# A new order of emission for the pieces of the first layer

## The chip, the cores and the metric

The kernel runs on one core of one Trainium2 chip. The metric is the device time of one execution in microseconds (us); the median of three runs is given. Times within an execution come from one profiled execution and count from its first instruction.

## The reference

Three stages follow each other. The first is a gated delta rule over 4 batches, 8 heads, 768 steps and 48 dimensions; its output becomes a matrix x of 3072 tokens by 384. The other two are MLP layers over that matrix.

```python
for t in range(S):
    y[:, :, t] = einsum('bhd,bhde->bhe', q[:, :, t], state)
    v_old = einsum('bhde,bhd->bhe', state, k_n[:, :, t])
    state = state + b[t] * einsum('bhd,bhe->bhde', k_n[:, :, t], v[:, :, t] - v_old)
h = maximum(x @ w_in, 0);  x = (h * h) @ w_out              # 384 -> 2048 -> 384
gate = 1 / (1 + exp(-(x @ w_gate)));  out = (gate * (x @ w_val)) @ w_out2   # 384 -> 1536 -> 384
```

The weights of both MLP layers arrive as 64-bit floats, which the kernel itself turns into pairs of 32-bit numbers.

## The kernel before

"First layer" is what one long list orders: the delta rule and the squared-ReLU MLP together, with the conversion of their weights. The sequence of 768 steps is cut into 12 chunks of 64 steps, handled in 6 groups (g = 0 to 5) of two chunks (st = 0 and 1). A group gives 512 token rows, on which the MLP runs with 16 slices of 128 hidden units.

Every piece of work is a Python function, and `ORDER` (lines 38 to 89) is a string of 961 tokens, "name,arguments". The loop `for token in ORDER.split(): run(token)` (line 775) calls them one after the other under a manual schedule. Nothing else orders the work: each engine, and SP's queue of DMAs, executes its own instructions in the order of emission, and an instruction whose input or buffer isn't ready holds back all that stand behind it on the same engine. The tokens:

- Loads, issued on SP: `kn`, `kt`, `kc`, `kz`, `q`, `v`, `k2` (keys, queries and values of a chunk in several layouts, two buffers each), `f` (64-bit weights of hidden slice f, 768 KB), `li` and `lw` (low parts of a slice's weights for the first and second product, read back from DRAM, three buffers each). `sl` stores the low part of a slice, `z` moves the rows of a chunk into token order by DMA, `po` stores a finished group.
- Norms: `sq` (ACT), `sm` (VectorE, L325), `no` (VectorE with a square root on ACT, L331 to L348). `sv` scales v on POOL (L312).
- Delta rule inside a chunk, on TensorE with evictions on VectorE or ACT: `a` (scores among keys, L363 and L367), `p` (scores against queries, L383 or L398); then the inversion of the triangular blocks: `ti` (memsets on POOL, a 32 by 32 transpose on VectorE, L439 and L441), `r,g,i` (three rows of the inversion each, on VectorE, L447 to L477), `to` and `t1` (transposes, L480 and L483), `ja`, `jb`, `jc` (joins of 16-row blocks, groups 0 and 1), `n` and `w` (joins of 32-row blocks).
- Across chunks, one after the other: `ks` (product with the state, L566 to L578), `t` (L584), `y` (output, L620 and L622), `s` (new state, L597 and L607). `x` splits the rows into a high and a low part (L125 on ACT, L126 on VectorE); the row buffer xr is single, so `z` of the next chunk waits for `x` of the one before.
- Weights of slice f: `hi` (ACT), `b` (VectorE, L148 and L152), `b2` (VectorE, L157 and L161), `lo` (POOL, L168), `ch` (ACT, L214), `cl` (POOL, L218). The buffer between `hi` and `cl` is double, so `hi` of a slice waits for `cl` of the one two before. `w2,i,k` are the same steps for weights of the second layer.
- MLP, n = 16 g + f: `h,n` is 9 matmuls of 512 columns (L681) and three ACT passes; `g,n` a subtraction on VectorE (L704); `o,n` 9 matmuls (L719), which need `g,n`. `h,16 g` needs both `x` of its group.
- `d,n` issues n matmuls that only keep TensorE busy.

PSUM holds three banks for the attention pieces; most of these take two. After the list, a loop ends the first layer (slices 82 to 95), and a second one computes the gated layer.

Of the kernel before, what the change touches and what calls it, by code (L numbers as in the profile page):

```python
# [59 lines left out]
sv,2,1 a,3,0 h,23 w,2,1 g,22 w2,0,3 lw,23 t,2,0 ti,3 ti,3,3 li,24 k2,2,1 o,21 h,25 w2,0,4 lw,22 g,23 y,2,0  # L60
ti,3,1 w2,1,0 q,2,1 lw,24 w2,1,1 r,3,0 g,25 kc,2,1 o,22 r,3,1 r,3,2 lw,27 h,24 g,24 s,2,0 o,23 li,27 h,27 li,26
r,3,3 g,27 ks,2,1 o,24 v,3,0 h,26 lw,25 z,2,0 r,3,4 x,2,0 o,25 li,28 t,2,1 g,26 h,28 y,2,1 kn,4,1 lw,26 o,26
li,34 li,29 sq,4,1 r,3,5 o,27 r,3,6 w2,0,5 h,29 r,3,7 lw,28 g,28 k2,3,0 sv,3,0 z,2,1 g,29 s,2,1 w2,1,2 w2,1,3
lw,29 li,30 h,30 x,2,1 kz,3,0 o,28 o,29 g,30 v,3,1 li,31 r,3,8 li,32 lw,30 kc,3,0 lw,32 p,3,0 h,31 g,31 r,3,9
r,3,10 h,32 w2,1,4 g,32 to,3 lw,33 o,30 h,34 kz,3,1 p,3,1 li,33 lw,31 o,31 h,33 sm,4,1 n,3,0 ks,3,0 w2,2,0
w2,2,1 li,36 g,33 kt,4,1 kt,4,0 no,4 li,35 t1,3 lw,34 o,32 a,4,0 w2,1,5 n,3,1 h,36 lw,35 o,33 g,34 k2,3,1 h,35
w2,2,2 a,4,1 w,3,0 w2,2,3 o,34 t,3,0 lw,36 g,35 g,36 li,37 w,3,1 ti,4 w2,2,4 ti,4,1 kc,3,1 li,38 ti,4,3 po,1
h,37 g,37 r,4,0 r,4,1 y,3,0 w2,3,0 o,35 h,38 r,4,2 o,36 g,38 s,3,0 lw,37 li,40 w2,3,1 r,4,3 h,40 r,4,4 sv,3,1
li,39 o,37 g,40 h,39 lw,38 z,3,0 g,39 o,38 kn,5,1 ks,3,1 sq,5,0 x,3,0 w2,2,5 lw,39 lw,40 li,42 w2,3,2 q,4,0
w2,3,3 h,42 o,39 sq,5,1 o,40 q,3,1 g,42 t,3,1 li,44 r,4,5 v,4,0 li,41 h,41 g,41 k2,4,0 lw,41 lw,44 li,43 r,4,6  # L70
y,3,1 h,43 g,43 r,4,7 lw,42 kc,5,1 o,41 o,42 sv,4,0 h,44 li,45 kz,4,0 g,44 li,46 lw,43 w2,3,4 p,4,0 w2,4,0 z,3,1
r,4,8 x,3,1 h,46 r,4,9 g,46 o,43 w2,3,5 h,45 g,45 s,3,1 o,44 li,50 w2,4,1 w2,4,2 lw,47 lw,45 r,4,10 w2,4,3 h,50
to,4 li,47 o,45 lw,46 h,47 g,47 t1,4 o,46 g,50 kz,4,1 li,49 p,4,1 sm,5,0 li,48 w2,4,4 n,4,0 lw,49 o,47 lw,50
sm,5,1 h,48 w2,4,5 lw,48 w2,5,0 w,4,0 g,48 kt,5,0 ks,4,0 h,49 o,48 li,51 li,52 lw,51 no,5 w2,5,1 t,4,0 g,49 h,52
o,49 kt,5,1 w2,5,2 li,53 w2,5,3 h,51 w2,5,4 a,5,0 po,2 g,51 v,4,1 li,55 sv,4,1 n,4,1 o,50 g,52 lw,54 a,5,1
w2,5,5 w,4,1 h,53 g,53 o,51 li,56 h,56 lw,52 o,52 ti,5 ti,5,3 w2,6,0 w2,6,1 g,56 w2,6,2 y,4,0 lw,53 kc,4,1
w2,6,3 o,53 li,54 q,4,1 z,4,0 ti,5,1 h,54 r,5,0 g,54 li,58 s,4,0 h,55 li,59 o,54 h,59 w2,6,4 w2,6,5 r,5,1 lw,56
g,55 r,5,2 lw,55 li,57 w2,7,0 w2,7,1 r,5,3 r,5,4 o,55 h,57 g,57 o,56 lw,57 w2,7,2 lw,58 h,58 lw,60 li,60 ks,4,1
o,57 g,59 h,60 g,58 t,4,1 o,58 v,5,0 li,61 li,66 lw,59 g,60 x,4,0 h,61 r,5,5 y,4,1 q,5,0 g,61 k2,5,0 li,62 o,59
w2,7,3 h,62 kz,5,0 r,5,6 o,60 p,5,0 g,62 li,65 lw,61 o,61 z,4,1 x,4,1 lw,64 w2,7,4 li,63 h,63 lw,62 w2,7,5 r,5,7  # L80
g,63 r,5,8 h,66 lw,63 o,62 li,64 li,70 kc,5,0 h,64 g,66 g,64 o,63 h,65 o,64 li,68 h,68 ks,0,0 g,65 lw,65 o,65
li,67 lw,66 h,67 g,67 o,66 w2,8,0 li,69 h,69 g,68 r,5,9 lw,67 w2,8,1 sv,5,0 o,67 h,70 li,74 r,5,10 lw,68 to,5
g,69 w2,8,2 o,68 g,70 k2,4,1 li,72 lw,71 lw,69 s,4,1 n,5,0 po,3 t1,5 lw,75 o,69 h,72 li,71 lw,70 w2,8,3 ks,5,0
n,5,1 w,5,0 li,73 w2,8,4 h,71 t,5,0 o,70 w2,9,0 g,72 h,74 y,5,0 g,71 o,71 h,73 g,73 q,5,1 li,76 w2,8,5 kz,5,1
p,5,1 li,75 lw,73 lw,72 w,5,1 o,72 o,73 lw,74 g,74 v,5,1 w2,9,1 w2,9,2 sv,5,1 w2,9,3 s,5,0 li,78 h,75 z,5,0 g,75
w2,9,4 w2,9,5 h,76 g,76 o,74 ks,5,1 o,75 w2,10,0 w2,10,1 h,78 lw,76 x,5,0 li,77 t,5,1 o,76 h,77 g,77 y,5,1 li,82
li,79 lw,78 h,79 lw,77 lw,79 o,77 g,78 li,81 w2,10,2 z,5,1 w2,10,3 g,79 li,80 x,5,1 w2,10,4 w2,10,5 w2,11,0
lw,80 o,78 lw,81 o,79 k2,5,1 h,80 lw,82 h,81 g,80 li,83 w2,11,1 w2,11,2 g,81 w2,11,3 w2,11,4 po,4
# [1210 lines left out]
```

## Time and profile before

| | |
|---|---|
| median of 3 runs | 1071.47 us (1062.65 to 1074.42) |
| the profiled execution | 1073.17 us, of which the span from the first to the last instruction is 1071.4 us |
| mean granted TensorE clock | 0.984 |
| TensorE busy | 1003.6 us (94%) |
| VectorE busy | 772.5 us (72%) |
| ACT, POOL busy | 463.2 us, 200.7 us |
| end of the first layer (its last o in the chain) | some 633 us |

Busy times are those of the engine's instructions; a matmul's end is modelled and overlaps the next. The granted clock is a share of full speed (1 is 2.4 GHz, 0.5 is 1.2 GHz). "Issue" as a releaser means that the engine waited for nothing that the profile shows. In the rows below, a bracket behind an instruction is the engine's idle time ahead of it and what ended that. A matmul of 32-bit floats counts as two instructions in attention pieces.

### The profile page before, as it was taken

The numbers are of one execution on the slowest core, as the hardware profiler recorded it, in microseconds if no ns is written. First come the engines' busy times: TensorE is split into PE (matmuls) and PEld (weight loads), VectorE is DVE, ScalarE is ACT, GpSimd is POOL, SyncE is SP. The second block draws the span as 40 slices with busy tenths as digits, with TensorE's granted clock in tenths as the row PEclk, the third lists the DMA queues.
The fourth block names the chain that finished last, engine by engine and source line by source line (L and its number), as shares of the span: only waits on it lengthen the run. The fifth ranks groups of instructions, "written<-read, shape, count | busy, mean of one in ns | idle before, by whom it ended". The sixth has DMA issues, their size and how long they took to land.

```text
span 1071.4 us, 27395 instructions
## 1 busy us (share of the span) xinstructions
PE 1003.6 (94%) x11607; PEld 821.8 (77%) x11611; DVE 772.5 (72%) x1460; ACT 463.2 (43%) x763; POOL 200.7 (19%) x157
## 2 busy tenths in 40 slices
...
GB/s 283 173 209 198 194 202 210 193 200 156 188 197 135 247 171 208 178 178 170 136 159 251 262 226 243 187 162 123 216 160 131 99 126 89 89 133 171 110 3 57
DMA packets 81803, 182.78 MB, mean 171 GB/s; under 512 B 22032, under 2 KB 54928, under 8 KB 77072
## 3 DMA queue, kind: packets, MB, share of 16 engines
...
## 4 chain that ended last, share of the span: by engine, by line
PE 81%; DVE 6%; issue 2%; DMA 2%; ACT 1%; POOL 1%; SPq 1%; DVEq 0%; ACTq 0%; POOLq 0%
PE h L681 18%; PE o L719 18%; PE gx L1140 12%; PE gy L1140 11%; PE o L1019 10%; PE r L1199 2%; DMA il<-w1d 2%; PE att L553 1%; PE att L584 1%; PE att L620 1%; PE att L566 1%; PE att L538 1%; PE att L622 1%; PE att L377 1%; PE att L363 1%
## 5 line engine op out<-in xcount | busy, mean ns | idle before, releaser
L704 DVE TENSOR_TENSOR gl<-gg,gh 128x512 fp32r<-128x512 f32 x96 | 73.5, 773 | 94.3 <-ACT gg L698 94.0
L695 ACT ACTIVATE gg<-h 128x512 f32<-128x512 f32 x96 | 57.4, 598 | 181.7 <-PE h L681 171.9
L719 PE MATMUL o<-gh,il 128*128 128x512 f32 x288 | 113.8, 395 | 1.2 <-DMA il<-w1d 1.2
L1019 PE MATMUL o<-gh,wo 128*128 128x512 f32 x270 | 93.0, 394 | 0.0
L719 PE MATMUL o<-gh,w1h 128*128 128x512 f32 x216 | 87.8, 406 | 0.0
L681 PE MATMUL h<-xhi,il 128*128 128x512 f32 x288 | 84.1, 401 | 2.3 <-DMA il<-w1d 2.3
L719 PE MATMUL o<-gl,w1h 128*128 128x512 f32 x216 | 85.7, 397 | 0.0
L1140 PE MATMUL gx<-xa,wg 128*128 128x512 f32 x288 | 76.7, 395 | 2.1 <-DVE valB L1052 1.2
L1140 PE MATMUL gy<-xa,wg 128*128 128x512 f32 x288 | 76.2, 393 | 0.0
L681 PEld LDWEIGHTS h<-xhi,il 128*128 128x128 f32 x288 | 55.6, 194 | 15.8 <-DMA il<-w1d 3.6
L681 PE MATMUL h<-xhi,w1h 128*128 128x512 f32 x216 | 66.3, 417 | 0.0
L1140 PEld LDWEIGHTS gx<-xa,wg 128*128 128x128 f32 x288 | 53.6, 188 | 16.4 <-DVE gateB L1052 2.3
L719 PEld LDWEIGHTS o<-gh,il 128*128 128x128 f32 x288 | 54.7, 190 | 12.6 <-DMA il<-w1d 1.9
L1140 PEld LDWEIGHTS gy<-xa,wg 128*128 128x128 f32 x288 | 53.7, 188 | 13.0 <-DVE gateC L1052 0.4
L681 PE MATMUL h<-xlo,w1h 128*128 128x512 f32 x216 | 62.0, 396 | 0.0
L698 ACT ACTIVATE gg<-gg 128x512 f32<-128x512 f32 x96 | 60.7, 632 | 3.1
L697 ACT ACTIVATE gh<-gg 128x512 fp32r<-128x512 f32 x96 | 60.7, 632 | 3.1
L168 POOL TENSOR_TENSOR y<-raw 128x768 f32<-128x768 f32 x12 | 19.7, 1643 | 217.7 <-DVE raw L161 167.3
L1019 PEld LDWEIGHTS o<-gh,wo 128*128 128x128 f32 x270 | 50.7, 188 | 11.9
L470 DVE TENSOR_TENSOR tt<-tt,tmp 128x40 f32<-128x40 f32 (+7 forms) x208 | 52.2, 285 | 1.5 <-DVE tmp L463 0.2
L1019 PE MATMUL o<-gl,wo 128*128 128x512 f32 x135 | 53.2, 394 | 0.0
L463 DVE TENSOR_TENSOR tmp<-xi,tt 128x40 f32<-128x40 f32 (+7 forms) x208 | 51.0, 279 | 1.3
...
## 6 DMA issues: line engine op xcount, KB each, us to landing
...
```

The lines of the kernel that those rows point to most:

```text
L168: nc.gpsimd.tensor_tensor(out=t, in0=c["t"], in1=c["raw"][:, :, 0].bitcast(F32), op=ALU.add)
L463: nc.vector.tensor_tensor(out=tv[i], in0=xi[:, 0:j, j].unsqueeze(2).to_broadcast([128, j, n]), in1=tt[:, j, lo:hi].unsqueeze(1).to_broadca ...
L470: nc.vector.tensor_tensor(out=tt[:, 0:j, lo:hi], in0=tt[:, 0:j, lo:hi], in1=tv[i], op=ALU.subtract)
L681: nc.tensor.matmul(out=ps[:, cs], lhsT=w[:, kc * 128:kc * 128 + 128], rhs=x[:, kc, cs], start=(i == 0 and kc == 0), stop=(i == 2 and kc == ...
L695: nc.scalar.activation(out=gg, in_=ps, func=ACTF.Relu)
L697: nc.scalar.activation(out=gh, in_=gg, func=ACTF.Square)
L698: nc.scalar.activation(out=gg, in_=gg, func=ACTF.Square)
L704: nc.vector.tensor_tensor(out=gl, in0=gg, in1=gh.bitcast(F32), op=ALU.subtract)
L719: nc.tensor.matmul(out=po[m], lhsT=w[:, cs], rhs=x, start=(f == 0 and i == 0), stop=(f == NF1 - 1 and i == 2),)
L1019: nc.tensor.matmul(out=po2[g, m], lhsT=w, rhs=x, start=start, stop=stop)
L1140: nc.tensor.matmul(out=ps, lhsT=a, rhs=c, start=k == 0 and u == us[0], stop=k == 2 and u == us[-1],)
L1199: nc.tensor.matmul(out=po_m, lhsT=x[:, cs], rhs=w, start=f == 0 and i == 0, stop=f == NF2 - 1 and i == 2)
```

## The change

The string `ORDER` is replaced by another order of the same 961 tokens, each as often as before. The first 31 tokens are the same (line 39 and line 40 up to r,0,4). The functions behind the tokens, buffers and the code after the list are the same. The parts that are spoken of below, old lines and then new ones:

```diff
 d,1 kn,0,0 sq,0,0 kn,0,1 sm,0,0 kt,0,0 sq,0,1 be sm,0,1 no,0 kt,0,1 d,1 a,0,0 cj kn,1,1 q,0,1 kc,0,1 f,0 a,0,1
-kn,1,0 k2,0,1 cs ti,0 ti,0,1 ti,0,3 kt,1,1 r,0,0 r,0,1 r,0,2 r,0,3 r,0,4 f,1 d,1 f,2 hi,1 hi,0 to,0 p,0,1 b,0
-b2,0 d,1 lo,0 sq,1,0 sq,1,1 ja,0,1 kc,0,0 sm,1,1 t1,0 ch,0 cl,0 ja,0,0 jb,0,0 b,1 k2,0,0 v,0,0 b2,1 hi,2 kt,1,0
-v,0,1 lo,1 ch,1 sm,1,0 kn,2,0 b,2 q,0,0 p,0,0 jc,0,0 sl,0 f,3 lw,0 cl,1 n,0,0 b2,2 kn,3,1 sl,1 no,1 a,1,0 sq,2,0
-lo,2 ch,2 sm,2,0 cl,2 li,0 sq,3,1 sv,0,0 hi,3 w,0,0 q,1,0 b,3 jb,0,1 f,5 hi,5 b2,3 lo,3 t,0,0 sm,3,1 n,0,1 f,4
-sl,2 b,5 b2,5 lo,5 a,1,1 ch,3 cl,3 v,1,0 hi,4 b,4 jc,0,1 kn,2,1 b2,4 li,2 s,0,0 w,0,1 sv,0,1 lo,4 ti,1 kt,2,0
-f,8 ks,0,1 ti,1,1 sv,1,0 ti,1,3 r,1,0 sl,3 ch,4 r,1,1 k2,1,0 y,0,0 f,6 z,0,0 r,1,2 cl,4 t,0,1 ch,5 x,0,0 sl,4
-y,0,1 kn,3,0 r,1,3 r,1,4 hi,6 to,1 kc,2,0 lw,2 z,0,1 d,1 b,6 x,0,1 b2,6 cl,5 lo,6 f,7 s,0,1 d,2 ja,1,1 hi,7 lw,1
-b,7 sq,2,1 sl,5 t1,1 ch,6 sq,3,0 cl,6 b2,7 h,0 ja,1,0 li,1 hi,8 g,0 h,1 lo,7 kc,1,0 sm,2,1 ch,7 b,8 jb,1,1 h,2
-o,0 li,4 f,9 g,1 o,1 sl,6 cl,7 b2,8 lo,8 li,3 kt,2,1 ks,1,0 hi,9 ch,8 h,3 li,5 f,10 sl,7 lw,3 g,2 q,1,1 b,9 h,5
-no,2 jb,1,0 cl,8 b2,9 n,1,1 hi,10 g,3 lw,6 lo,9 o,2 li,6 h,4 b,10 ch,9 f,11 g,4 o,3 sl,8 p,1,0 cl,9 hi,11 kn,4,0
-b2,10 sm,3,0 sq,4,0 lw,4 lw,5 jc,1,1 lo,10 b,11 ch,10 li,7 g,5 h,6 kc,1,1 o,4 sl,9 a,2,1 li,8 b2,11 n,1,0 f,12
-cl,10 jc,1,0 hi,12 lo,11 ch,11 li,9 g,6 b,12 sl,10 cl,11 o,5 w,1,0 a,2,0 h,7 b2,12 g,7 o,6 f,13 hi,13 b,13 w,1,1
-b2,13 li,10 lo,12 t,1,0 lw,7 o,7 lo,13 ti,2 ti,2,3 ti,2,1 sl,11 lw,9 ch,12 cl,12 h,9 v,1,1 sv,1,1 h,8 g,8 y,1,0
...
-g,15 p,2,1 h,17 g,16 g,17 w2,0,1 o,15 r,2,7 v,2,0 li,18 r,2,8 h,18 li,20 lw,17 g,18 k2,2,0 li,21 o,16 o,17 h,20
-li,19 h,19 r,2,9 lw,18 g,20 g,19 o,18 h,21 r,2,10 sv,2,0 lw,19 kt,3,1 kn,5,0 q,2,0 lw,20 o,19 to,2 t1,2 li,25
-kc,4,0 ks,2,0 n,2,0 v,2,1 li,23 o,20 no,3 n,2,1 li,22 a,3,1 h,22 kt,3,0 g,21 q,3,0 lw,21 po,0 w,2,0 w2,0,2
...
+kn,1,0 k2,0,1 cs ti,0 ti,0,1 ti,0,3 kt,1,1 r,0,0 r,0,1 r,0,2 r,0,3 r,0,4 sq,1,0 v,0,0 sv,0,0 to,0 q,0,0 v,0,1
+sv,0,1 hi,0 d,1 d,1 f,1 kt,1,0 hi,1 k2,0,0 d,1 p,0,1 b,0 b2,0 ja,0,0 sm,1,0 lo,0 ch,0 ja,0,1 kc,0,0 cl,0 b,1 f,2
+hi,2 kn,3,1 sl,0 t1,0 sq,1,1 b2,1 lo,1 ch,1 cl,1 p,0,0 b,2 jb,0,0 b2,2 sq,3,1 f,3 hi,3 lo,2 ch,2 jb,0,1 n,0,0
+jc,0,0 sm,1,1 b,3 b2,3 no,1 f,4 n,0,1 sl,1 sm,3,1 cl,2 f,5 hi,5 b,5 w,0,0 a,1,1 kn,3,0 lo,3 sq,3,0 sl,2 ch,3
+cl,3 jc,0,1 q,1,0 li,1 hi,4 t,0,0 sm,3,0 kc,1,0 b2,5 li,0 b,4 w,0,1 b2,4 lo,4 ch,4 a,1,0 f,6 sl,3 kn,2,1 ti,1
+cl,4 ti,1,1 f,7 lo,5 s,0,0 sq,2,1 sl,4 hi,6 ks,0,1 b,6 ch,5 lw,0 ti,1,3 y,0,0 v,1,1 z,0,0 t,0,1 cl,5 sl,5 r,1,0
+r,1,1 r,1,2 x,0,0 y,0,1 b2,6 d,2 lw,3 r,1,3 lo,6 s,0,1 r,1,4 f,8 z,0,1 kn,2,0 x,0,1 hi,7 li,4 ch,6 cl,6 to,1
+sq,2,0 b,7 b2,7 hi,8 p,1,0 k2,1,0 h,0 lo,7 ja,1,0 b,8 f,9 t1,1 ch,7 b2,8 h,1 ja,1,1 sl,6 cl,7 g,0 g,1 hi,9 h,4
+li,5 sm,2,0 lo,8 ch,8 b,9 kt,2,0 o,0 f,10 sl,7 cl,8 b2,9 li,2 lo,9 jb,1,0 lw,1 kt,2,1 sm,2,1 o,1 q,1,1 hi,10
+ch,9 sl,8 jb,1,1 lw,2 n,1,0 b,10 b2,10 no,2 li,3 h,2 g,2 a,2,0 cl,9 f,11 lo,10 n,1,1 g,4 hi,11 b,11 ch,10 h,3
+v,1,0 o,2 jc,1,0 sl,9 cl,10 b2,11 jc,1,1 a,2,1 g,3 lw,4 f,12 w,1,0 hi,12 sl,10 b,12 h,5 sv,1,0 ks,1,0 li,6 lo,11
+ch,11 b2,12 cl,11 lw,5 o,3 kc,1,1 li,8 w,1,1 t,1,0 ti,2 ti,2,1 f,13 lo,12 hi,13 h,8 b,13 b2,13 kz,2,0 p,1,1 li,7
+o,4 lo,13 ch,12 g,8 h,6 sl,11 g,5 li,9 ti,2,3 lw,6 g,6 cl,12 y,1,0 ch,13 r,2,0 o,5 kc,2,0 f,14 p,2,0 hi,14 b,14
+b2,14 o,6 lw,8 r,2,1 h,7 g,7 s,1,0 r,2,2 sl,12 h,9 g,9 lw,7 z,1,0 x,1,0 v,2,0 o,7 o,8 r,2,3 sv,1,1 li,10 cl,13
...
+h,15 g,15 li,16 w2,0,0 h,16 r,2,9 r,2,10 kt,3,0 w2,0,1 h,17 s,1,1 to,2 li,21 g,16 lw,15 o,15 lw,17 li,19 h,19
+ks,2,0 n,2,0 li,18 o,16 g,17 po,0 no,3 a,3,0 t1,2 n,2,1 h,18 g,18 o,17 kt,3,1 a,3,1 lw,18 w,2,0 g,19 w2,0,2 h,21
+lw,19 w2,0,3 w2,0,4 w,2,1 ti,3 q,2,1 li,23 ti,3,1 li,20 kc,3,0 v,3,0 ti,3,3 r,3,0 kn,4,0 r,3,1 t,2,0 lw,23 o,18
+o,19 lw,21 kz,3,0 g,21 lw,20 y,2,0 w2,1,0 h,20 li,22 g,20 r,3,2 w2,1,1 kc,2,1 s,2,0 h,23 o,20 li,25 li,24 r,3,3
...
+ks,3,0 n,3,0 v,3,1 w2,2,5 o,31 w,3,0 sm,4,1 no,4 a,4,0 li,34 g,33 q,3,0 h,34 g,34 lw,32 o,32 a,4,1 w,3,1 ti,4
```

Some of what differs: sv,0,0 and sv,0,1 stand ahead of to,0 and hi,0. POOL's order lo,3 lo,5 cl,3 sv,0,1 lo,4 becomes lo,3 cl,3 lo,4 ti,1 cl,4 lo,5. ja,1,1 stands behind h,1 rather than ahead of h,0, and p,1,0 ahead of h,0. The conversion of slices 13 and 14, the transposes and first rows of group 2 and p,1,1 and p,2,0 stand ahead of g,7. Loads of group 3 are spread over more tokens.

## Rows read from the trace of the kernel before

**Rows 1.** Busy time by stretch: the first layer in three parts (engines PE, PEld, DVE, ACT, POOL)
```profile
core 0: us, PE busy (x) PEld busy (x) DVE busy (x) ACT busy (x) POOL busy (x), PEclk, DMA share, GB/s
0.00:98.30 98.30, 53.09 (x1926) 47.87 (x1930) 80.38 (x136) 35.45 (x57) 39.43 (x46) 0.96 0.70 211
98.30:210.30 112.00, 107.41 (x2103) 86.74 (x2092) 100.18 (x168) 64.59 (x104) 43.08 (x24) 0.94 0.68 208
210.30:640.00 429.70, 420.99 (x5750) 344.35 (x5749) 291.98 (x681) 228.13 (x373) 44.45 (x34) 0.98 0.64 189
```

**Rows 2.** Waits of VectorE from 31.4 to 156 us, and its busy time there
```profile
engine line waited for: us in total, times, longest us
DVE y L148 <- ACT wt L143: 4.4, 3, 3.5
DVE gl L704 <- ACT gg L698: 2.9, 2, 1.5
DVE rn L336 <- ACT n L334: 2.6, 2, 2.1
DVE ks L574 <- PE att L566: 2.1, 1, 2.1
DVE pm L398 <- PE att L392: 1.5, 2, 1.3
DVE am L367 <- PE att L363: 1.4, 1, 1.4
...
31.40:156.00 124.60, 97.05 (x2891) 83.65 (x2893) 105.80 (x149) 64.22 (x106) 54.74 (x30) 0.92 0.63 193
```

**Rows 3.** Timeline up to the first MLP product (start us, us, engine, line)
```profile
90.62 0.96 DVE L126 TENSOR_TENSOR xlo<-xr,xhi 128x768 fp32r<-128x768 f32 x1
...
95.89 0.83 ACT L125 CAST xhi<-xr 128x768 fp32r<-128x768 f32 x1 [7.58 <-DMA xr<-yt]
...
97.15 1.26 PE L499 MATMUL att<-t,am 32*16 32x16 f32 x128 [8.20 <-DVE t L480]
...
98.34 1.65 PE L681 MATMUL h<-xhi,w1h 128*128 128x512 f32 x3
```

**Rows 4.** Groups of VectorE by line: xcount, busy us, mean ns, idle before
```profile
L152 DVE SCALAR_TENSOR_TENSOR wt<-wt,y 128x768 uint32<-128x768 uint32 x16 | 16.8, 1052 | 1.5
L148 DVE TENSOR_SCALAR y<-wt 128x768 uint32<-128x768 uint32 x16 | 15.4, 963 | 4.4 <-ACT wt L143 4.4
L157 DVE TENSOR_SCALAR y<-wt 128x768 uint32<-128x768 uint32 x16 | 10.7, 670 | 0.3
L161 DVE SCALAR_TENSOR_TENSOR raw<-raw,y 128x768 f32<-128x768 uint32 x19 | 18.2, 959 | 0.7
L470 DVE TENSOR_TENSOR tt<-tt,tmp 128x40 f32<-128x40 f32 (+7 forms) x208 | 52.2, 285 | 1.5 <-DVE tmp L463 0.2
L463 DVE TENSOR_TENSOR tmp<-xi,tt 128x40 f32<-128x40 f32 (+7 forms) x208 | 51.0, 279 | 1.3
L439 DVE STREAM_TRANSPOSE xi<-am 128x1024 f32<-128x1024 f32 x6 | 12.0, 1998 | 3.8 <-PE att L553 3.7
L383 DVE TENSOR_TENSOR pm<-att,mask 128x512 f32<-128x512 f32 x16 | 10.2, 681 | 0.5 <-PE att L377 0.5
```

**Rows 5.** Timeline: a row of the inversion beside a POOL instruction
```profile
86.94 1.82 POOL L218 TENSOR_TENSOR wl<-wt,w1h 128x768 fp32r<-128x768 f32 x1 [5.66 <-DMA w1d<-wl]
87.04 1.87 DVE L450 TENSOR_TENSOR tmp<-xi,tt 128x126 f32<-128x126 f32 x1
```

**Rows 6.** Timeline and chain: g,7; o,7's start; two h; one s piece
```profile
154.96 1.04 DVE L704 TENSOR_TENSOR gl<-gg,gh 128x512 fp32r<-128x512 f32 x1 [1.46 <-ACT gg L698]
...
157.14 0.50 PE L719 MATMUL o<-gh,w1h 128*128 128x512 f32 x1
...
159.48 4.08 PE h L681 x18
...
167.78 1.15 PE L597 MATMUL att<-u,k 64*64 64x48 f32 x64
```

**Rows 7.** The stop inside a,3,1, and the busy table around it
```profile
237.08 1.87 PE L363 MATMUL att<-kt 48*64 48x64 f32 x63 [2.42 <-issue]
...
225.00:236.00 11.00, 9.66 (x220) 7.79 (x218) 9.02 (x20) 6.42 (x10) 2.53 (x3) 1.00 1.00 274
235.00:240.00 5.00, 2.92 (x66) 2.61 (x67) 1.03 (x2) 0.68 (x2) 0.00 (x0) 0.75 0.14 47
```

More of the change, by code (lines that the diff above doesn't have):

```diff
@@ L49 @@
-no,2 jb,1,0 cl,8 b2,9 n,1,1 hi,10 g,3 lw,6 lo,9 o,2 li,6 h,4 b,10 ch,9 f,11 g,4 o,3 sl,8 p,1,0 cl,9 hi,11 kn,4,0
-b2,10 sm,3,0 sq,4,0 lw,4 lw,5 jc,1,1 lo,10 b,11 ch,10 li,7 g,5 h,6 kc,1,1 o,4 sl,9 a,2,1 li,8 b2,11 n,1,0 f,12
-cl,10 jc,1,0 hi,12 lo,11 ch,11 li,9 g,6 b,12 sl,10 cl,11 o,5 w,1,0 a,2,0 h,7 b2,12 g,7 o,6 f,13 hi,13 b,13 w,1,1
-b2,13 li,10 lo,12 t,1,0 lw,7 o,7 lo,13 ti,2 ti,2,3 ti,2,1 sl,11 lw,9 ch,12 cl,12 h,9 v,1,1 sv,1,1 h,8 g,8 y,1,0
-kz,2,0 f,14 ch,13 g,9 r,2,0 hi,14 b,14 h,10 lw,8 s,1,0 sl,12 o,8 o,9 b2,14 cl,13 sm,4,0 ks,1,1 z,1,0 li,11 x,1,0
```

62 lines of the change are left out of this document (30 added, 32 removed).

## The prediction

> **What bounds the kernel now.** I read the busy time by stretch first, then what TensorE and VectorE waited for, and last the timeline around the first MoE product. In the busy table the reader is to see three stretches of the first layer [rows 1]. Up to 98.3 us, where token h,0 starts, TensorE is busy 53.1 of 98.3 us: 45 us are lost, and VectorE (80.4 us) carries the stretch. From 98.3 to 210.3 us TensorE loses 4.6 us of 112 and its granted clock averages 0.94; VectorE is busy 100 of 112 us, so both are near their ends. From 210.3 to 640 us TensorE is busy 421.0 of 429.7 us. The list moves no work in or out, so its effect on the end of the layer is the change in TensorE's lost time: its idle time, and what a lower clock stretches.
>
> VectorE's waits between 31.4 and 156 us add up to 4.4 + 2.9 + 2.6 + 2.1 + 1.5 + 1.4 = 14.9 us [rows 2]. The rest of its 18.8 us of idle time there (124.6 - 105.8), 3.9 us, is gaps between its 149 instructions, 0.026 us each, which no order takes away.
>
> **How h,0 comes to start at 98.34 us** [rows 3]. x,0,0's subtraction starts at 90.62 and takes 0.96 us; it frees the one xr buffer, the row DMAs z,0,1 go out, and x,0,1's cast starts at 95.89 and takes 0.83 us: 5.1 us from the end of one to the end of the other, 96.72. h,0 could start there, but ja,1,1 stands ahead of it on TensorE and waits for the transpose to,1 until 97.15.
>
> **The change, part by part.** *The start.* To r,0,4 the two lists are the same tokens. Between there and x,0,0 the new list gives VectorE sm,3,0 and b,6 more and sm,2,0 less: b is one tensor_scalar and one scalar_tensor_tensor, 0.96 + 1.05 = 2.0 us [rows 4]. It takes away two waits: POOL's order lo,3 lo,5 cl,3, which held cl,3, and so hi,4, back until b2,5 was done (3.5 us of the row y <- wt), becomes lo,3 cl,3 lo,4; and no,1 comes after b,3, so that the square root on ACT should be reached (2.1 us of the row rn <- n) [rows 2]. I take 5 us of waits gone and 1 us new (ks,0,1 follows s,0,0's eviction on ACT, which now stands behind ch,4). So xlo(0,0) ends at 91.6 + 2.0 - 5 + 1 = 89.6 and h,0 starts at 94.7, for ja,1,1 is no longer ahead of it: p,1,0 is, whose inputs are loaded long before. That is 3.6 us earlier. If POOL's lo and ch still hold hi,4 back, it is 98; if nothing is waited for, 93.7.
>
> *scale_v moved forward.* sv,0,0 and sv,0,1 on POOL go from behind cl,2 and cl,3 to a place ahead of lo,0, so that they run once v has landed, which I take to be beside group 0's rows on VectorE. A row that meets a POOL tensor_tensor can wait for its end: L450 took 1.87 us beside one of 1.82 us, where its neighbours take some 0.3 [rows 5]. Two such meetings cost up to 2 x 1.6 = 3.2 us, or nothing if v lands while the transposes before the rows run; the meetings that the same two had in their old places, of the same price at most, go. The balance lies between -3.2 and +3.2 us; I take +1, since the rows are many and short, and the old neighbours longer.
>
> *From h,0 to o,7: VectorE's work is pulled ahead.* This speaks against the change. Before g,7, counted from the start, the new list has on VectorE all that the old one has, and besides ti,2 ti,2,1 ti,2,3 (3 x 2.0 us), b and b2 of chunks 13 and 14 (2 x (0.96 + 1.05 + 0.67 + 0.96) = 7.3), p,1,1 and p,2,0 (4 x 0.68 = 2.7), g,8 (0.8) and r,2,0 r,2,1 (2 of the 44 row tokens of groups 2 to 5 that share 51.0 + 52.2 us: 4.7): 21.5 us [rows 4]. 40 instructions add 1.0 us of gaps. g,7 ended at 156.0 us [rows 6]. With all waits gone and w new ones it ends at 156.0 + 21.5 + 1.0 + 1 - 14.9 + w = 164.6 + w. TensorE, for its part, has six tokens more done before o,7 (h,8 h,9 at half of 4.08 us each, p,1,1 p,2,0 s,1,0 at 1.1, y,1,0 with twice the matmuls at 2.1: 9.5 us). The old list started o,7 at 157.1 [rows 6], so it had that much done at 166.6. The gain at o,7 is thus 166.6 - 164.6 - w = 2.0 - w: the 3.6 us of the start are mostly paid back, because o,7 needs g,7. w lies between 0 and the 14.9 of before; as VectorE now runs behind TensorE rather than ahead of it, its inputs are there when it comes, and I take w = 0.5, near the lower end. Gain 1.5 us. Past o,7 TensorE has no wait of the same kind to 200 us, so this gain stays.
>
> *The stop at 234 us.* TensorE stood 2.42 us inside a,3,1, waiting for nothing that the profile shows, while the DMA engines were busy at a share of 1.00; its granted clock was 0.75 in the 5 us around it, a mean over its two levels (1.2 and 2.4 GHz) [rows 7]. In the old list the loads kt,3,0 and q,3,0 and the store po,0 of a group's output stand within eight tokens there, and n,2,1 a,3,1 follow ks,2,0 n,2,0 with one o between. In the new one kt,3,0 is issued before h,17 and q,3,0 not before g,33, and a,3,0 n,2,1 come with h,18 and o,17 behind them. I take this stop as gone: 2.4 us, and 5 x 0.25 = 1.3 us of clock, 3.7 us. Ends: nothing, if stops fall anywhere in instruction-dense pieces (the new list has 16 places with two or more attention pieces in a row after h,17, the old one 15), and minus as much again if one more comes. The Trainium skill, "Runtime: NRT & Kernel Launch", section "Instruction fetch mechanics", has the sequencer refill instructions in blocks through its own DMA queue, a cost that it calls mostly hidden. The stop in a busy DMA stretch goes against "hidden"; by the page there would be nothing for the list to move, and the sum would end 3.7 us higher.
>
> *The rest.* From o,20 on each pair is a reshuffle with the same sets within a few us; loads il keep three buffers, and their waits (some 0.3 to 1 us each) I cost at nothing, hidden by TensorE's queue of h and o; without that cover each late one costs 1 us. The second layer has no edit.
>
> **Sum.** 1.5 + 3.7 = 5.2 us. The profiled execution took 1073.2 us (span 1071.4), which gives 1068.0; the median of the runs shown, 1071.5, lies 1.7 us lower, so I forecast **1066** for a median.
>
> **Rivals.**
> 1. *The stops go altogether.* From 210 to 640 us 8.7 us are idle and the clock's mean of 0.98 stretches some 8 us more [rows 1]. If the new spacing removes three quarters of these 17 us (12.7) and w is 0 (2.0), the time is 1071.5 - 14.7, near 1057. For it: only a handful of stops hold most of that time. Against it: 16 dense places for 15.
> 2. *Nothing moves.* The stops stay, the start is paid back whole: 1071. For it: the lost time of the old list before o,7 is VectorE's, and VectorE gets more to do there. Against it: 14.9 us of waits are to be had, and the new order does the waiting work later.
> 3. *VectorE becomes the bound between o,5 and o,16: slower.* Mechanism: the rows and weight chunks pulled ahead of g,7 are themselves late, because hi and ch on ACT wait for POOL, as cl,3 did. Every us that VectorE waits before g,7 then goes to the end, for TensorE has nothing else queued. With w = 14 (the waits of before, moved) the gain at o,7 is -12; with the stop at 234 us staying, the time is 1071.5 + 12 = 1083; with half of the waits, w = 7, it is 1076. It decides from w = 2 on if no stop goes, from w = 5.7 if the one does. For it: the share of VectorE is already 0.89 there, and the slack of every g before its o shrinks. Against it: a stall of VectorE in the old list often was one for TensorE, which ran ahead less.
>
> **How the numbers follow.** The forecast (1061 to 1071) has 0.44, rival 1 0.29, rival 2 0.11, rival 3 0.16. A measurement of this kernel can tell about 1% from no change, 10.7 us (its three runs spread over 11.8 us). Faster by over 1%, below 1060.8: most of rival 1 (0.25) and the forecast's edge (0.06), 0.31. Slower by over 1%, above 1082.2: half of rival 3 and a little, 0.10. Within: 0.59. The range runs from 1053 (rival 1 with nearly all 17 us) to 1079 (rival 3 with w near 9); about 0.1 lies on each side. The likeliest case's own range is 1061 to 1071.
>
> **What would show it.** Right: h,0 starts at 93.7 to 96 us; in VectorE's waits the row y <- wt falls from 4.4 to under 1.5 us before o,7; o,7 starts within 4 us of 164.6; VectorE's busy share from h,0 to o,7 is above 0.93; the stop inside a,3,1 is gone and the clock holds 1.00 there. Wrong: h,0 at 98 us or later (the start's step); o,7 after 168 us (rival 3); a stop of over 2 us in another dense piece (the late step); or idle time of TensorE from 210 to 640 us under 4 us (rival 1).

## The result, and the profile after

The new list takes **1084.3 us** (median of six runs, 1081.6 to 1086.9); beside it the list of before took 1069.5 us (1062.7 to 1077.3). The ratio is 1.0123, with an interval of 1.0093 to 1.0153. That is some 13 us slower, where I forecast 1066 us: outside the range, and on the side that I gave a chance of 0.10. The profiled execution took 1084.7 us, with a span of 1083.0.

The busy table of the new list, cut at the same three tokens as [rows 1] and with its columns (h,0 now starts at 102.5 us, o,15 at 226.0):

```profile
0.00:102.50 102.50, 55.54 (x1865) 48.90 (x1865) 86.32 (x137) 39.06 (x62) 42.03 (x47) 0.61 0.72 209
102.50:226.00 123.50, 108.98 (x2158) 86.50 (x2156) 109.53 (x202) 61.43 (x101) 41.81 (x23) 0.93 0.65 190
226.00:652.00 426.00, 420.00 (x5754) 343.94 (x5751) 291.46 (x646) 228.07 (x373) 43.31 (x34) 0.99 0.64 189
```

At o,15 both lists have given TensorE the same work, and the new one gets there 15.7 us later. TensorE's idle time up to there grew by 11.7 us: from 45.2 to 47.0 us ahead of h,0, and from 4.6 to 14.5 us between h,0 and o,15. Its busy time grew by 4.0 us (160.5 to 164.5) for the same matmuls, those that ran at a lower granted clock among them. Behind o,15 the new list is no worse: 6.0 us idle, 8.7 before. The loss is made by 226 us, and most of it between h,0 and o,15.

The granted clock up to h,0 was 0.61 in this execution and 0.96 before, but the loss doesn't hang on that: of the six runs of the new list, the two with a mean clock of 0.950 and 0.953 took 1084.7 and 1081.6 us, and the four with 0.984 to 0.987 took 1082.9 to 1086.9 us.

What TensorE waited for from 102.5 to 226 us (columns: us in total, times, longest):

```profile
PE o L719 <- DVE gl L704: 8.2, 4, 3.2
PE h L681 <- DMA il<-w1d: 2.6, 1, 2.6
PE att L553 <- issue: 2.3, 1, 2.3
```

The first row did not exist before: four times an o stood and waited for VectorE's g. VectorE itself, from 31.4 us to the end of g,7 (181.7 us now, 156.0 before), which answers to [rows 2]:

```profile
DVE y L148 <- ACT wt L143: 3.4, 2, 2.8
DVE ks L574 <- PE att L566: 1.9, 1, 1.9
DVE am L367 <- PE att L363: 1.8, 1, 1.8
DVE rn L336 <- ACT n L334: 0.6, 2, 0.3
DVE wt L152 <- DVE y L148: 0.5, 1, 0.5
DVE xlo L126 <- DMA w1s<-in_w_dram: 0.2, 1, 0.2
...
31.40:181.73 150.33, 113.04 (x3296) 94.97 (x3296) 137.27 (x178) 74.95 (x123) 62.09 (x36) 0.73 0.61 187
```

Its waits fell from 14.9 to 8.4 us, but its busy time up to the same token rose from 105.8 to 137.3 us. That is 31.5 us more, where I had counted 21.5. Where the other ten come from is seen in the same instructions' mean times. From 31.4 us to g,7, the list of before:

```profile
L157 DVE TENSOR_SCALAR y<-wt 128x768 uint32<-128x768 uint32 x13 | 9.0, 695 | 0.2
L704 DVE TENSOR_TENSOR gl<-gg,gh 128x512 fp32r<-128x512 f32 x8 | 7.5, 932 | 2.9 <-ACT gg L698 2.9
```

and the new list:

```profile
L157 DVE TENSOR_SCALAR y<-wt 128x768 uint32<-128x768 uint32 x15 | 13.6, 907 | 0.3
L704 DVE TENSOR_TENSOR gl<-gg,gh 128x512 fp32r<-128x512 f32 x9 | 12.3, 1380 | 0.0
L470 DVE TENSOR_TENSOR tt<-tt,tmp 128x31 f32<-128x31 f32 (+5 forms) x6 | 4.8, 804 | 0.2
L463 DVE TENSOR_TENSOR tmp<-xi,tt 128x31 f32<-128x31 f32 (+5 forms) x6 | 1.6, 260 | 0.1
```

The same subtraction of g took 0.93 us on the mean before and takes 1.38 now. The timeline just ahead of g,7 shows what stretches a row of the solve:

```profile
170.89 1.84 POOL L218 TENSOR_TENSOR wl<-wt,w1s 128x768 fp32r<-128x768 f32 x1 [2.12 <-DMA w1d<-wl]
170.90 1.91 DVE L470 TENSOR_TENSOR tt<-tt,tmp 128x60 f32<-128x60 f32 x1
...
173.13 0.25 DVE L470 TENSOR_TENSOR tt<-tt,tmp 128x87 f32<-128x87 f32 x1
...
177.77 1.84 POOL L168 TENSOR_TENSOR wt<-wt,raw 128x768 f32<-128x768 f32 x1 [5.04 <-DVE raw L161]
177.91 1.83 DVE L470 TENSOR_TENSOR tt<-tt,tmp 128x112 f32<-128x112 f32 x1
...
181.78 0.50 PE L719 MATMUL o<-gl,w1h 128*128 128x512 f32 x1 [3.21 <-DVE gl L704]
```

A row that takes 0.25 us alone takes 1.8 to 1.9 us when it starts beside a POOL tensor_tensor of 1.84 us. Two of them stand ahead of g,7 and cost 3.2 us together, and the last line shows TensorE waiting 3.21 us for that g. It is the meeting of [rows 5], more often and in a place where TensorE waits for it. The Trainium skill, "SBUF — State Buffer", section "Who interferes with whom", says that a VectorE instruction with two SBUF inputs and a GpSimd (POOL) instruction that reads SBUF lock each other out, the later one for the whole of the other; the 1.91 us beside 1.84 agree with that.

The start, which answers to [rows 3]:

```profile
92.93 0.96 DVE L126 TENSOR_TENSOR xlo<-xr,xhi 128x768 fp32r<-128x768 f32 x1
...
95.58 1.81 DVE L454 TENSOR_TENSOR tt<-tt,tmp 128x120 f32<-128x120 f32 x1
...
97.97 0.83 ACT L125 CAST xhi<-xr 128x768 fp32r<-128x768 f32 x1 [6.43 <-DMA xr<-yt]
98.51 1.70 DVE L607 TENSOR_TENSOR state<-state,att 128x384 f32<-128x384 f32 x3
99.11 3.47 PE L392 MATMUL att<-q,kc 48*64 48x64 f32 x60 [6.52 <-DVE state L607]
...
102.51 1.65 PE L681 MATMUL h<-xhi,w1h 128*128 128x512 f32 x3
```

x,0,0's subtraction comes at 92.93 (90.62 before), and x,0,1's cast ends at 98.80, 4.9 us behind the subtraction's end, as the 5.1 of [rows 3] let expect. But p,1,0, which the new list has ahead of h,0, stands 6.52 us: it needs two of the three PSUM buffers of the attention, and s,0,1 holds two until VectorE has added them to the state, behind a row stretched to 1.81 us. h,0 starts at 102.51. In the profiles of four kernels below whose tokens up to h,0 are the same, it starts at 100.3 to 101.5 us, so up to 2.2 of the 4.2 us belong to this one execution.

### The profile page after: what moved, and what is told of

It is laid out like the page before. It is cut to its first block, busy times and chain, and to the rows that moved or that the text cites. A ratio compares the mean times of both kernels' runs of the same rounds, so it can differ in the third digit from the quotient of the medians.

```text
span 1083.0 us, 27402 instructions
## 1 busy us (share of the span) xinstructions
PE 1006.2 (93%) x11611; PEld 821.8 (76%) x11611; DVE 785.8 (73%) x1460; ACT 463.6 (43%) x763; POOL 201.1 (19%) x157
## 4 chain that ended last, share of the span: by engine, by line
PE 76%; DVE 15%; issue 3%; DMA 3%; ACT 1%; SPq 1%; POOL 1%; DVEq 0%; ACTq 0%; POOLq 0%
PE h L681 16%; PE o L719 16%; PE gx L1140 11%; PE gy L1140 11%; PE o L1019 10%; PE r L1199 2%; PE att L553 1%; PE att L363 1%; DVE xi L441 1%; DVE tt L470 1%; PE att L584 1%; DVE gl L704 1%; PE att L566 1%; DVE y L148 1%; DVE wt L152 1%
## 5 line engine op out<-in xcount | busy, mean ns | idle before, releaser
L719 PEld LDWEIGHTS o<-gl,w1h 128*128 128x128 f32 x216 | 41.0, 190 | 18.6 <-DVE gl L704 9.9
L463 DVE TENSOR_TENSOR tmp<-xi,tt 128x40 f32<-128x40 f32 (+7 forms) x208 | 53.3, 289 | 1.4
```

The lines of the kernel that those rows point to most:

```text
L463: nc.vector.tensor_tensor(out=tv[i], in0=xi[:, 0:j, j].unsqueeze(2).to_broadcast([128, j, n]), in1=tt[:, j, lo:hi].unsqueeze(1).to_broadca ...
L719: nc.tensor.matmul(out=po[m], lhsT=w[:, cs], rhs=x, start=(f == 0 and i == 0), stop=(f == NF1 - 1 and i == 2),)
```

## The experiments

Times of one batch are compared with the list of before on the same chip; medians of before were 1068.9 to 1070.4 us. In four kernels (the g's moved, the solve moved together with p,2,0, p,1,0 moved, the late part alone) the line numbers of the profile are one lower.

**Only the g's moved.** Theory V was that VectorE's total is the bound, theory G that the g's merely stand too late.

```diff
-... h,0 lo,7 ja,1,0 b,8 ... h,1 ja,1,1 sl,6 cl,7 g,0 g,1 ...
+... h,0 g,0 lo,7 ja,1,0 b,8 ... h,1 g,1 ja,1,1 sl,6 cl,7 ...
```

> The new list with eight g tokens (0, 1, 3, 4, 5, 6, 7, 8) moved up to stand right behind their own h; nothing else moves. Theory V (VectorE's total up to g,15, its instructions stretched beside POOL included, sets the stretch from h,0 to o,15): the four waits of o for gl, 8.2 us, shrink but the work that stood ahead of the g's is late next; o,15 starts at 222 to 226 us (226.0 in the new list) and the time is 1081 to 1085 us. Rival G (only the g's stand too late): the 8.2 us go whole and are not paid back; o,15 near 217 us, time 1075 to 1077 us.

Measured: 1082.8 us, ratio 1.011 (1.0072 to 1.0149), 1.6 us under the new list and within its noise. TensorE's waits from 101.5 to 227 us:

```profile
PE o L718 <- DVE gl L703: 3.1, 1, 3.1
...
PE att L510 <- DVE xi L482: 1.3, 1, 1.3
...
PE att L498 <- DVE t L479: 1.1, 1, 1.1
PE att L583 <- DVE v L577: 0.9, 2, 0.7
```

The wait for g fell from 8.2 to 3.1 us, and waits for VectorE's other results took its place (xi, t, v). o,15 came at 227.2 us, 1.2 us behind the new list's. G falls: the g's place is not the cause, the work that somebody must wait for is.

**The group-2 solve put back**, first with p,2,0, then alone.

```diff
-o,3 ... t,1,0 ti,2 ti,2,1 ... ti,2,3 ... r,2,0 o,5 kc,2,0 f,14 p,2,0 ... o,6 lw,8 r,2,1 h,7 g,7
+o,7 ti,2 ti,2,1 ti,2,3 o,8 r,2,0 ... o,9 r,2,1 r,2,2 ... g,12 r,2,3 r,2,4 ...
```

> The new list with the group-2 solve put back behind the products it was pulled ahead of: ti,2 ti,2,1 ti,2,3 behind o,7, r,2,0 to r,2,6 behind o,8 to g,13, p,2,0 behind g,11. Theory V: VectorE has some 12 us less ahead of g,7, fewer short rows meet POOL's tensor_tensors, and TensorE has no more waits for gl from o,5 to o,7; but the rows have to be done before o,16 all the same, so about half is paid back there: o,7 at 168 to 172 us (178.0), time 1075 to 1080 us. Rival G as in the other run (only the place of the g's matters, and they get free here too): 1075 to 1077 us with o,7 near 170. Rival S (the loss is made before h,0 and by the half clock there): o,15 stays within 2 us of 226, time 1082 to 1085 us.

> The new list with the group-2 solve alone put back (ti,2 ti,2,1 ti,2,3 behind o,7, r,2,0 to r,2,6 behind o,8 to g,13); p,2,0 stays in its new place. Theory B (VectorE's work pulled ahead of the g's is what costs): o,7 starts near 174 us as it did with p,2,0 moved too, the wait of 8.9 us for p,2,0's buffers does not come, and of the 5 to 6 us won at o,9 about half is left at o,15: time 1077 to 1081 us. Rival T (VectorE's total up to g,15 is what costs, wherever its parts stand): o,15 stays at 224 to 228 us, time 1082 to 1086 us.

With p,2,0 moved: 1090.4 us, ratio 1.0188 (1.0148 to 1.0227), worse than the new list and outside what each of the three theories gave. o,7 started at 174.5 us (178.0 in the new list) and o,9 at 182.1 us (188.9), but then a new wait gave back more than that:

```profile
196.77 1.28 DVE L382 TENSOR_TENSOR pm<-att,mask 128x512 f32<-128x512 f32 x2
197.50 1.94 PE L583 MATMUL att<-v,t 64*64 64x48 f32 x60 [8.90 <-DVE pm L382]
```

t,1,1 needed PSUM buffers that p,2,0 held, whose eviction stood on VectorE behind the rows just put there. With the solve alone moved: 1081.5 us, ratio 1.0117 (1.0086 to 1.0147). o,9 came at 182.6 us, 6.3 us earlier, but o,15 at 224.9, only 1.1 earlier, as rival T has it, and TensorE's wait for g was 9.3 us. Work moved behind one product is in the way of the next: it is the total that counts. The median lies 2.8 us under the new list's, between the two forecasts, but the ratio, taken on the same chip, only 0.0006 under.

**p,1,0 behind h,0.**

```diff
-hi,8 p,1,0 k2,1,0 h,0 ... o,2 jc,1,0
+hi,8 k2,1,0 h,0 ... o,2 p,1,0 jc,1,0
```

> The new list with p,1,0 moved from ahead of h,0 to behind o,2, near its old place. TensorE stood 6.5 us in it, waiting for VectorE's eviction of s,0,1, which holds two of the three PSUM buffers. Theory V: h,0 starts at 99 us instead of 102.5 (the cast of x,0,1 ends at 98.8), but g,7 and o,15 hang on VectorE, so o,15 moves by 2 us at most and the time is 1082 to 1085 us. Rival S (the late start of h,0 is carried to the end): time 1079 to 1081 us.

Measured: 1089.6 us, ratio 1.019 (1.0146 to 1.0234). Both missed. h,0 starts at 96.65 us, earlier than before the change, and nothing is won: TensorE then waits inside h,0 for VectorE's half of x.

```profile
96.65 1.65 PE L680 MATMUL h<-xhi,w1h 128*128 128x512 f32 x3 [6.72 <-ACT xhi L124]
...
102.28 1.65 PE L680 MATMUL h<-xlo,w1h 128*128 128x512 f32 x3 [2.70 <-DVE xlo L125]
```

So h,0 is done at 103.9 us. In the run with the new start and the loads of before (below), p,1,0 stands 6.53 us in its place ahead of h,0, and h,0 is done at 103.85 us (its last three matmuls start at 103.00 and take 0.85 us). The 6.5 us that p,1,0 stood thus cost nothing by themselves there, and an earlier h,0 is not a gain as long as VectorE is late. Why the list with p,1,0 moved is 5 us worse than the new list stays open; its profiled run was the fastest of its four (1082.3 us).

**The late part alone.** The list of before up to o,15, then the new order.

```diff
 ... g,17 w2,0,1 o,15
-r,2,7 v,2,0 li,18 r,2,8 h,18 ...
+v,2,0 k2,2,0 sv,2,0 q,2,0 r,2,7 r,2,8 ...
```

> The list of before up to o,15, and behind it what is left, in the order of the new list. In the two profiles o,15 starts 15.7 us later in the new list and the first layer ends 12.4 us later, so the late part would be 3.3 us shorter. Theory L (the late part of the new list is better by itself): the time is 3 us under the kernel before, ratio 0.995 to 0.999. Rival N (the late part only had slack to catch up after a late VectorE): ratio 0.999 to 1.003. Rival W (instruction-dense places of the new list cost more stops): ratio above 1.003.

Measured with 12 runs: 1070.7 us, ratio 1.0005 (0.9976 to 1.0033). The late part is worth less than some 3 us either way. Rival N fits this best: the 3.3 us that the new list made up in its profile would then be slack behind a late o,15. That there is such slack is argued, not shown.

**VectorE relieved, in both lists.** First POOL's work on the chunks nearly taken away, so that little stretches VectorE; then VectorE's own b left out for ten chunks.

```diff
-out=t, in0=c["t"], in1=c["raw"][:, :, 0].bitcast(F32), op=ALU.add
+out=t[:, 0:32], in0=c["t"][:, 0:32], in1=c["raw"][:, 0:32, 0].bitcast(F32), op=ALU.add
...
-nc.gpsimd.tensor_tensor(out=wl_t[f], in0=wt_t.pop(f), in1=w1h[f].bitcast(F32), op=ALU.subtract)
+wl_t[f] = w1h[f]
... (the second relief, in b)
+if not all_:  # chunks 6 to 15
+    return
```

> The list of before, with POOL's work on the weight chunks nearly gone: the add of lo runs over 32 of 768 columns, and cl's subtraction is left out (the low part of w1 that is stored is a copy of the high part), so the products use other numbers. It is the base for the next run. All theories: VectorE's short instructions are no longer stretched to 1.8 us beside a POOL tensor_tensor (14.8 us of it from h,0 to o,15), and time falls by 0 to 12 us against the kernel before.

> The same two edits in the new list (lo's add over 32 columns, cl's subtraction left out, so the products use other numbers). Theory V (the new list loses because VectorE, the bound from h,0 to o,15, is stretched by 11 us more beside POOL): the new list is at most 5 us behind the list of before with the same edits. Rival B (VectorE's backlog as such: g's, PSUM evictions and the solve stand behind work pulled ahead, stretched or not): still 8 to 15 us behind. Rival P (TensorE's own stops for nothing that shows and the half clock after them, which the order of the attention pieces makes): 10 us or more behind.

> The list of before, with VectorE's two instructions of b left out for weight chunks 6 to 15 (some 2.0 us each, 20 us of VectorE; these chunks get other numbers). Base for the next run. All theories: 0 to 15 us under the kernel before, since VectorE's share from h,0 to o,15 falls from 0.89 to some 0.75.

> The new list with the same two instructions left out for chunks 6 to 15 (these chunks get other numbers). Theory V and rival B (VectorE is the bound there, stretched or not): with 20 us taken from VectorE the new list is at most 5 us behind the list of before with the same edit. Rival P (TensorE's own stops and half clock): 10 us or more behind.

| kernel | list of before | new list |
|---|---|---|
| as it is | 1 | 1.0123 (1.0093 to 1.0153) |
| POOL's chunk work short | 0.9998 (0.9973 to 1.0024) | 1.0047 (1.0009 to 1.0085) |
| b left out for chunks 6 to 15 | 0.9990 (0.9966 to 1.0015) | 1.0048 (1.0020 to 1.0076) |
| b's first instruction three times (next runs) | 1.0127 (1.0087 to 1.0166) | 1.0230 (1.0185 to 1.0275) |

Either relief leaves the list of before where it was and takes some 8 us by the ratios from the new one (medians 1084.3 to 1074.8 and 1074.2 us). In the new list with POOL's work short, VectorE's lines up to 180 us read:

```profile
L157 DVE TENSOR_SCALAR y<-wt 128x768 uint32<-128x768 uint32 x15 | 8.3, 555 | 0.3
L148 DVE TENSOR_SCALAR y<-wt 128x768 uint32<-128x768 uint32 x15 | 8.3, 554 | 13.8 <-ACT wt L143 13.7
L704 DVE TENSOR_TENSOR gl<-gg,gh 128x512 fp32r<-128x512 f32 x10 | 7.3, 747 | 0.0
```

g is back at 0.75 us and L157 at 0.56, and VectorE now has time to wait (13.8 us ahead of L148). TensorE's row of waits for g is gone there; what is left of its idle time are stops for nothing that shows and a load:

```profile
PE att L499 <- issue: 3.5, 1, 3.5
PE att L553 <- issue: 2.6, 1, 2.6
PE att L363 <- issue: 2.2, 1, 2.2
PE h L681 <- DMA il<-w1d: 1.9, 1, 1.9
```

V predicted at most 5 us left between the lists in both pairs; B predicted 8 to 15 us with POOL's work short and at most 5 us with b left out. By the ratios 5.2 (0.49%) and 6.2 us (0.58%) are left, each give or take 4 to 5 us. V comes nearest, B's 8 us are not excluded, and rival P's 10 us or more lie at the very end of what the intervals allow. These runs do not part V from B cleanly: short POOL work also brings the chunks earlier, and leaving b out relieves a backlog of any kind.

**VectorE loaded, in both lists.**

```diff
-nc.vector.tensor_scalar(out=c["y"], in0=d, scalar1=4, ...)
+for _ in range(times):  # 3 for chunks 6 to 15
+    nc.vector.tensor_scalar(out=c["y"], in0=d, scalar1=4, ...)
```

> The list of before, with the first instruction of b (0.55 us, the row y<-wt) issued three times instead of once for chunks 6 to 15: 20 more instructions, some 12 us of VectorE, the same numbers. Theory T (only the new list has VectorE at its bound; in the old one VectorE has 10 us to spare from h,0 to o,15): 1 to 6 us slower, ratio 1.001 to 1.006. Rival U (both lists stand at VectorE's bound): 9 to 13 us slower, ratio 1.008 to 1.012.

> The new list with the same 20 instructions more. Theory T and rival U: 9 to 14 us slower than the new list, ratio to before 1.020 to 1.026. Rival W (the new list's loss is no matter of VectorE's total): at most 4 us slower than the new list, ratio to before up to 1.016.

1083.2 and 1093.8 us: 13.7 us on the list of before and 9.5 on the new one. The line with the added instructions, L148, was busy 17.9 us more in the profile of the one (33.3 against 15.4 us) and 14.4 us more in the other (30.3 against 15.9), not 12. T was wrong about the old list, and U, whose 9 to 13 us are just passed, right in kind: there is nothing to spare. Less work on VectorE wins nothing there, more costs most of it. The old list stands at the knee, a point from which only the one direction changes the time, and with this load it lands where the new list is. In the new list the wait for g alone rose from 8.2 to 14.4 us:

```profile
PE o L719 <- DVE gl L704: 14.4, 4, 6.8
PE att L392 <- DVE state L607: 7.7, 1, 7.7
```

**The dense run of attention pieces.**

```diff
-n,1,0 ... h,2 g,2 a,2,0 ... n,1,1 ... h,3 ... o,2 jc,1,0 ... jc,1,1 a,2,1 ... w,1,0 ... h,5 ... o,3
+h,2 g,2 n,1,0 ... h,3 a,2,0 ... o,2 n,1,1 h,5 jc,1,0 ... o,3 li,8 jc,1,1 a,2,1 h,8 w,1,0 ... o,4 w,1,1
```

> The new list with the attention pieces between o,0 and o,4 spread out: n,1,0 a,2,0 n,1,1 jc,1,0 jc,1,1 a,2,1 w,1,0 w,1,1 stand one or two at a time between h and o tokens (h,5 and h,8 moved up), and ti,2 ti,2,1 follow w,1,1 behind o,4. Theory P (besides VectorE's 10 us, the dense run of pieces costs 5 us: the stops of 0.6 and 2.3 us in which TensorE waits for nothing that shows, and h,2 and h,5 at half clock behind them): TensorE's lost time from o,0 to o,3 falls from 13 to some 7 us; time 1077 to 1080 us. Rival V (VectorE's backlog decides and takes the gain back): 1082 to 1086 us.

> The same spreading, with VectorE relieved (b left out for chunks 6 to 15, these chunks get other numbers), to be set beside the new list with b left out (ratio 1.0048 to before). Theory P: what is left there, 5 to 6 us, is the dense run; the ratio falls to 0.998 to 1.001. Rival S (what is left is the start and waits for loads): ratio stays at 1.004 to 1.006.

1081.8 us, ratio 1.0125 (1.0075 to 1.0175): no difference that can be told, and o,7 at 179.8 us (178.0). With VectorE relieved 1.0035 (1.0010 to 1.0059) against 1.0048 (1.0020 to 1.0076): the intervals overlap. Both fall between the forecasts; theory P, as far as it has a price, has one too small for these runs.

**Start or middle.** A first splice had a fault of its own:

```diff
-(the new start: li,1 ... li,0 ... lw,0 ... lw,3 ... li,4 ... p,1,0 k2,1,0) h,0 lo,7 ja,1,0 b,8 f,9 ...
+(the same start) h,0 sm,2,0 v,1,0 li,2 kt,2,0 sv,1,0 kc,2,0 lw,2 ja,1,1 lw,1 t1,1 ja,1,0 g,0 h,1 ...
```

> The new list up to h,0 and behind it what is left, in the order of before. Theory M (the loss is made between h,0 and o,15, not in the start, since o,0 comes only some 2 us later in the new list): ratio to before 0.999 to 1.004, with h,0 near 102 us as in the new list. Rival S (the late start of VectorE, x,0,1 at 103.4 instead of 98.5 us, is carried through): 4 to 8 us slower, ratio 1.004 to 1.008.

1083.2 us, ratio 1.0127 (1.0091 to 1.0164), but not for the reason in question. The loads came in another order than the products that free their buffers, and SyncE's queue stood behind one of them:

```profile
SPq L659 <- PE o L719: 17.0, 1, 17.0
...
112.00:116.00 4.00, 3.52 (x11) 2.28 (x10) 3.90 (x5) 0.00 (x0) 0.00 (x0) 0.50 0.01 4
```

With the DMA share at 0.01 for some 12 us nothing can be read from it. The two that tell the parts apart keep the loads in the order of use:

> The new list up to h,0, with its five loads il and ol replaced by those that the list of before has first, and behind it what is left, in the order of before. Theory M (the loss is made behind h,0): ratio to before 0.999 to 1.004. Rival S (VectorE's later start, x,0,1 some 3 to 5 us later and more work left for it, is carried through): ratio 1.004 to 1.008.

> The list of before up to h,0 (its first loads il and ol replaced by those of the new list), and behind it what is left, in the new list's order, with p,1,0 behind h,1. Theory M: nearly the whole loss is there, ratio 1.008 to 1.013. Rival S: ratio 1.003 to 1.007, since VectorE has 5 us less to catch up.

New start, then the order of before: 1075.6 us, ratio 1.0050 (1.0019 to 1.0081). Start of before, then the new order: 1078.0 us, ratio 1.0092 (1.0059 to 1.0124). The first is the figure of S, the second that of M: neither theory holds alone. Both parts lose, 5 us and 8 to 10 us, and their sum (1.4%) is the whole (1.2%) within its noise. None of the runs points to a list that beats the old one: relief of VectorE did not help it.

## Why the prediction was wrong

**The start (forecast: h,0 at 94.7 us, 3.6 earlier; came: 102.5, 4.2 later; the run with the new start: 5 us slower).** Two terms failed. I let 5 us of VectorE's waits go against 1 us new, and put 2.0 us of work in. Up to the end of x,0,0's subtraction its idle time fell by 1.2 us only and its busy time rose by 3.5 us (the list of before, then the new one; the third pair of numbers is VectorE):

```profile
31.40:91.58 60.18, 41.93 (x1603) 38.70 (x1605) 51.88 (x74) 26.80 (x46) 27.97 (x17) 0.99 0.60 187
31.40:93.89 62.49, 42.32 (x1607) 38.55 (x1607) 55.42 (x77) 28.50 (x48) 23.96 (x14) 0.52 0.60 184
```

So the subtraction ended at 93.9 instead of 89.6 us; the wait at y <- wt, which was to fall under 1.5 us, was still 3.4 us. And I put p,1,0 ahead of h,0 at nothing because its inputs were loaded; I did not ask which PSUM buffers were free. That wait, though, only covered VectorE's lateness: moved away, it gained nothing.

**From h,0 to o,7 (forecast: g,7's end at 164.6 + w with w = 0.5, o,7 within 4 us; came: 181.7, and o,7 at 178.0).** This is the step that decided. The form of the sum was right: 156.0 + 31.5 more of busy time - 5.7 less of idle time gives 181.8. Its terms were not. *Busy time:* I priced the pulled-ahead instructions at the means of the old list and left all the others as they were. g took 4.0 us more than I had counted (12.3 against 7.5, where I had 0.8 for one more), L157 3.3 us more (13.6 against 9.0, where I had 1.3 for two more), and the twelve row instructions of group 2 1.7 us more (4.8 + 1.6 for 4.7). That is 9.0 of the missing ten; the rest is the balance of smaller changes. Against their means with POOL short, g (1.38 over 0.75) and L157 (0.91 over 0.56) carry 9 x 0.63 + 15 x 0.35 = 11.0 us of stretch in the new list, and 8 x 0.185 + 13 x 0.14 = 3.3 us in the old. *Waits:* w came out as 8.4, not 0.5. (The 40 added instructions of my sum were 29, 178 for 149, which is 0.3 us.)

**The marker of the busy share (above 0.93 from h,0 to o,7)** came out at its edge and misled me: VectorE was busy 73.6 of 79.2 us from h,0 to the end of g,7, 0.93.

```profile
102.51:181.73 79.22, 67.32 (x1631) 53.14 (x1629) 73.58 (x89) 43.08 (x71) 34.49 (x20) 0.92 0.62 186
```

I had read a full VectorE as one that no longer wastes time; it was the bound.

**The stop at 234 us (forecast: -3.7 us).** The stop in a,3,1 is gone, as foretold, and others are there. From 226 to 652 us:

```profile
PE h L681 <- issue: 2.2, 2, 1.5
PE att L363 <- issue: 1.6, 1, 1.6
PE att L538 <- issue: 1.5, 2, 0.8
PE att L553 <- issue: 0.5, 1, 0.5
```

These sum to 5.8 us, and to 6.0 (2.4 + 2.3 + 1.3) in the list of before from 210 to 640 us. The late part alone measured 1.0005. The end that I gave as "nothing, if stops fall anywhere in instruction-dense pieces" was the right one.

My reason, the loads and the spacing around a,3,1, was not. Where the stops fall can be counted: from one stop of 0.35 us or more to the next TensorE executes 253 to 256 matmuls and weight loads, or a multiple of that. Between the places of the stops that end at 63.02 (a short one, 0.26 us) and 68.37 us in the list of before:

```profile
63.00:68.35 5.35, 3.94 (x127) 3.65 (x128) 4.49 (x6) 2.56 (x5) 2.15 (x2) 1.00 0.84 258
```

In all eighteen profiles there are 225 of these stops from 30 to 660 us. Divide the matmuls and weight loads counted ahead of each by 256: the remainder slides slowly from 187 near 35 us to 105 near 530 us and is, within a dozen, the same in every profile at the same count, so all 225 stand on one grid. The stop ahead of the last 63 matmuls of a,3,1 is there, 1.1 to 3.2 us long, in all six profiles that have the old order behind h,0; with the new start and the loads of before it reads:

```profile
242.56 1.96 PE L363 MATMUL att<-kt 48*64 48x64 f32 x63 [1.89 <-issue]
```

So an order decides which instruction stands at such a place, not how many places there are, and here the sum stayed at some 6 us. Nor did the clock hold 1.00 at a,3,1: it was 0.84 from 240 to 245 us. The sentence of the Trainium skill that I set against it ("Runtime: NRT & Kernel Launch", "Instruction fetch mechanics": refill costs mostly hidden) would also have left the list nothing to move, and the trace agrees with that much, by the 5.8 and 6.0 us. The even spacing fits a refill in blocks; that it is one, and what makes a stop long, short or absent, no run here shows.

**The rivals.** Rival 3 happened, near its price (1083 us with w = 14), at its place (o,5 to o,16 is part of it, o,0 onward is more exact), and by another path than I wrote, so that it is luck that the price came out near (w was 8.4, and the ten us of busy time did the rest): not chunks late because of hi and ch, but VectorE's own instructions, longer and more of them ahead of each product. I gave it 0.16 because I weighed whether VectorE would *wait*; what weighs is whether TensorE needs VectorE's result sooner than VectorE can have done everything listed ahead of it. What is shown: some 8 of the 13 us go when VectorE is relieved, by either way. Whether the stretch beside POOL or the backlog as such does it is not shown. What stays open too is the other 5: the stops, the loads il, and the half clock behind them are there in the trace, but the two runs that spread the pieces out told nothing. The stops from h,0 to o,15 sum to 10.2 us in the new list with POOL's work short and to 2.7 in the list of before with it, and to 5.5 and 3.9 with b left out; these are single executions. With POOL's work short, the four of ten runs with a mean clock of 0.947 to 0.953 took 1075.5 to 1080.9 us and the six with 0.987 to 0.993 took 1067.1 to 1077.6, so a half clock at the start may be part of it there; with b left out the runs don't split that way.
